# A transformer block on one core: one row of warm-up matmuls made longer, and part of the second layer norm moved between engines

## The chip, the cores and the metric

The kernel runs on one core of a Trainium2 chip. The metric is the device time of one execution, in microseconds (us). A profile of an execution also gives a span, from the first to the last instruction of the core; the device time is about 1.8 us longer than the span. The two must not be mixed.

Engines are named as in the profile: PE is TensorE (matmuls), PEld its weight loads, DVE VectorE, ACT ScalarE, POOL GpSimd, SP the engine that issues most DMAs.

## The reference, cut to what matters

```python
def reference(x, c, wqkv, wo, w_mod, w_fc1, w_fc2):     # B, N, D = 2, 256, 1152
    mod = (_silu(c) @ w_mod).reshape(B, 6, 1, D)
    shift_a, scale_a, gate_a, shift_m, scale_m, gate_m = [mod[:, i] for i in range(6)]
    h = _layernorm(x, axis=-1) * (1 + scale_a) + shift_a
    ...                                                  # q, k, v, attention, wo
    x = x + gate_a * a
    h2 = _layernorm(x, axis=-1) * (1 + scale_m) + shift_m      # "LN2"
    m = _gelu(h2 @ w_fc1) @ w_fc2                              # "FC1", "FC2"
    return x + gate_m * m
```

The 512 rows are four tiles (0 to 3) of 128; tiles 0 and 1 are batch 0, tiles 2 and 3 batch 1.

## The kernel before

At the start TensorE waits for the first weights (`w_scale_a`). A row of matmuls on zeros fills the wait and is meant to have its clock up when the work comes. In the profile of this kernel the row's matmuls start 0.43 us apart until the clock is released at 6.97 us, and 0.22 us apart from then on.

```python
    warm(2, pwarm)
    nc.tensor.transpose(pc[:], c_sb[:], ident[...])      # waits for c to land
    ...
    warm(14, pwarm)                                      # 128x128 by 128x512, on zeros
    act_stats()
    ...
    add0 = scale_group(0)                                # the first matmuls on w_scale_a
    ...
    k_step(0, 0, P)                                      # the first matmuls of K
```

In the second half each tile's `wo` output is gated (VectorE), added to x (GpSimd or VectorE), measured (VectorE), normalised, transposed by a DMA and modulated in place. The instructions stand on each engine in the order in which they are written here.

```python
    def ln2_modulate(b):
        for k in range(KD):                              # KD = 9 slices of 128 channels
            h = hT[:, k, b * N:(b + 1) * N]
            if k % 3 in ((1, 2) if b == 0 else (2,)):
                nc.scalar.activation(h, h, ACT.Identity, bias=shift_m[...], scale=scale_m[...])
            else:
                nc.vector.tensor_scalar(h, h, scale_m[...], shift_m[...], op0=ALU.mult, op1=ALU.add)

    def wo_group(t, i):                                  # tile t, column group i
        ...                                              # 9 matmuls into pacc
        nc.vector.tensor_tensor(tmp[:], pacc[:], gate_a[:, b, c0:c1], op=ALU.mult)
        (nc.gpsimd if i < 2 or t % TPB == 0 else nc.vector).tensor_tensor(
            x1[:, t, c0:c1], tmp[:], x_sb[:, t, c0:c1], op=ALU.add)
    ...
    ln2_stats(2, 1)
    ln2_modulate(0)
    wo_group(3, 0)
    ln2_stats(2, 2)
    ln2_sqrt(2)
    ...                                                  # the rest is in the diff below
    MSPLIT = 8
    for b in range(B):                                   # FC1: 8 panels for batch 0, then for batch 1,
        for m0 in range(0, MSPLIT, 2):                   # later panels for both batches at once
            ...
            if b == 0 and m0 == MSPLIT - 2:
                ln2_modulate(1)
```

## Time and profile before

| | before |
|---|---|
| timed runs, median of the first 3 | 245.29 us (245.05 to 245.33) |
| the profiled execution: device time | 246.9 us |
| the profiled execution: span | 245.04 us |
| TensorE busy | 97% of the span |

From the page of the kernel before. The last two lines cut the span into 40 slices: busy tenths of TensorE, and the clock that was granted to TensorE, in tenths of full speed.

```profile
span 245.0 us, 3884 instructions
...
PE 237.3 (97%) x1637; PEld 140.3 (57%) x1648; DVE 84.5 (34%) x198; ACT 65.5 (27%) x127; POOL 30.7 (13%) x46
...
PE   8789999999999999999999999999999999999994
...
PEclk9889999999999999999999999999999999999999
```

TensorE is the limit everywhere, and the two slices with a clock of 8 (6 to 18 us) stand out. The table of stretches shows them closer. Columns: stretch, its length, busy time of PE, PEld, DVE, ACT and POOL with the number of instructions, then the granted clock, the DMA share and GB/s.

```profile
8.00:9.00 1.00, 0.01 (x1) 0.02 (x2) 0.03 (x1) 0.00 (x0) 0.00 (x0) 1.00 1.10 352
10.00:11.00 1.00, 0.70 (x7) 0.57 (x7) 0.97 (x4) 0.65 (x3) 0.00 (x0) 0.69 1.15 323
11.00:12.00 1.00, 1.00 (x12) 1.00 (x10) 1.00 (x4) 1.00 (x4) 0.00 (x0) 0.50 1.11 334
12.00:13.00 1.00, 0.78 (x8) 0.72 (x8) 0.64 (x3) 0.77 (x2) 0.00 (x0) 0.50 1.20 306
13.00:14.00 1.00, 1.00 (x24) 1.00 (x24) 0.00 (x0) 0.00 (x0) 0.00 (x0) 0.60 1.16 316
```

TensorE idles from 8 to 9 us, and from 10.4 to 13.8 it runs at half clock. The waits of TensorE:

```profile
PE pm L221 <- DMA w_scale_a<-in_w_mod_dram: 1.2, 1, 1.2
...
PE pacc L706 <- DVE hT L599: 0.5, 1, 0.5
```

The first is the idle time at the start. The second is FC1's switch from batch 0 to batch 1, which waits for the modulates of batch 1. The timeline shows the VectorE work in front of it (start, duration, engine, line, operation, output and inputs):

```profile
96.62 1.20 DVE L599 TENSOR_SCALAR hT<-hT,scale_m,shift_m 128x256 bf16<-128x256 bf16 x3
...
99.89 8.02 PE L706 MATMUL pacc<-hT,w_f 128*128 128x256 bf16 x72
...
100.57 0.42 DVE L618 TENSOR_TENSOR x<-tmp,x_sb 128x256 f32<-128x256 f32 x1
...
101.69 0.29 DVE L618 TENSOR_TENSOR x<-tmp,x_sb 128x128 f32<-128x128 f32 x1
...
102.55 0.26 DVE L566 BATCH_NORM_AGGREGATE mv<-stats 128x2 f32<-128x24 f32 x1
...
108.41 5.81 PE L706 MATMUL pacc<-hT,w_f 128*128 128x256 bf16 x47 [0.50 <-DVE hT L599]
```

L599 are three modulates of batch 0, the two L618 are adds of tile 3, L566 aggregates tile 3's statistics. FC1 started at 99.89, so the aggregate began 2.66 us after it; the text calls this point the end of the statistics. Normalisation, transpose and modulates follow, and TensorE ran out of batch 0 before they were done.

### The profile page before, as it was taken

Reading aid. Unit: us, or ns where it says so; the run is one execution under the profiler, and the core shown is the slowest. Engines: PE = TensorE matmul, PEld = TensorE weight load, DVE = VectorE, ACT = ScalarE, POOL = GpSimd, SP = SyncE. Lnnn points to the kernel's source line nnn. Section 1 sums busy time; section 2 is a strip of 40 time slices with the busy share of each in tenths; the row PEclk is TensorE's granted clock in tenths of the full one; section 3 lists DMA queues with packets and bytes.
Section 4 is the critical chain, followed back from the end, with each engine's and each line's share of the span. In section 5 each row is a group of like instructions: output and inputs, shape, how many; then the busy total and the mean of one; then the engine's idle time right before and its main releaser. Section 6 shows DMA issues by size and latency. Waiting matters only on the chain.

```text
span 245.0 us, 3884 instructions
## 1 busy us (share of the span) xinstructions
PE 237.3 (97%) x1637; PEld 140.3 (57%) x1648; DVE 84.5 (34%) x198; ACT 65.5 (27%) x127; POOL 30.7 (13%) x46
## 2 busy tenths in 40 slices
PE   8789999999999999999999999999999999999994
PEld 2486444466666676878444444444665565566574
DVE  3752551214644677820000009999102000000001
ACT  7532351133524074482223322223000000000000
POOL 1000004000310514300000000000313221111111
PEclk9889999999999999999999999999999999999999
DMA  6999999999989972279999999999791000000000
GB/s 222 328 333 361 369 326 320 357 359 338 365 208 348 344 199 48 42 183 331 326 329 304 224 223 339 329 328 277 229 293 46 16 19 16 16 20 18 29 17 19
DMA packets 70813, 53.89 MB, mean 220 GB/s; under 512 B 18939, under 2 KB 65419, under 8 KB 70795
## 3 DMA queue, kind: packets, MB, share of 16 engines
q1 hardware_dynamic: 70064, 52.43, 72.9%
q0 software_dynamic: 704, 1.20, 1.6%
q8 instruction: 13, 0.21, 0.4%
q14 instruction: 5, 0.04, 0.1%
q10 hardware_dynamic: 27, 0.00, 0.0%
HBM read 48.08 MB, written 1.19 MB: 201 GB/s over the span
## 4 chain that ended last, share of the span: by engine, by line
PE 89%; DMA 4%; DVE 4%; issue 1%; ACT 1%; SPq 0%; DVEq 0%; ACTq 0%
PE pacc L766 29%; PE pacc L706 25%; PE pacc L503 7%; PE pacc L438 7%; PE pacc L612 6%; PE pk L253 5%; DMA w_scale_a<-in_w_mod_dram 3%; PE pk L282 2%; PE pn L365 1%; PE ps_s L458 1%; PE pa L530 1%; DMA hT<-xn 1%; PE pt L231 1%; DVE stats L624 1%; PE pm L221 1%
## 5 line engine op out<-in xcount | busy, mean ns | idle before, releaser
L706 PE MATMUL pacc<-hT,w_f 128*128 128x512 bf16 (+1 forms) x390 | 70.5, 340 | 0.8 <-DVE hT L599 0.5
L766 PE MATMUL pacc<-w_f,gT 128*128 128x384 bf16 (+2 forms) x468 | 70.5, 314 | 0.1
L766 PEld LDWEIGHTS <-gT 128*128 128x128 bf16 x468 | 44.3, 98 | 26.3
L706 PEld LDWEIGHTS <-w_f 128*128 128x128 bf16 x396 | 38.6, 98 | 32.4 <-issue 1.2
L429 DVE SCALAR_TENSOR_TENSOR late<-w_gate_mT,late 128x1152 bf16<-128x1152 bf16 x18 | 24.4, 1357 | 37.6 <-DMA w_gate_mT<-in_w_mod_dram 37.0
L772 DVE TENSOR_TENSOR tmp<-pacc,gate 128x384 f32<-128x384 f32 (+2 forms) x13 | 6.7, 525 | 63.0 <-PE pacc L766 50.5
L743 ACT ACTIVATE gT<-pacc 128x512 bf16<-128x512 f32 x28 | 16.7, 597 | 37.7 <-PE pacc L706 36.3
L612 PE MATMUL pacc<-w_o,big 128*128 128x384 bf16 (+2 forms) x117 | 18.1, 314 | 0.0
L503 PE MATMUL pacc<-w_v,hT 128*128 128x384 bf16 x108 | 17.9, 327 | 0.0
L774 POOL TENSOR_TENSOR o_sb<-tmp,x 128x384 bf16<-128x384 f32 (+1 forms) x12 | 11.6, 972 | 48.1 <-DVE tmp L772 48.1
L438 PE MATMUL pacc<-hT,w_q 128*128 128x512 bf16 x80 | 17.6, 380 | 0.1
L612 PEld LDWEIGHTS <-big 128*128 128x128 bf16 x117 | 10.9, 98 | 7.1 <-DVE big L270 0.6
L253 PE MATMUL pk<-big,w_k 128*128 128x256 bf16 (+2 forms) x88 | 14.2, 311 | 0.5 <-ACT big L240 0.4
L503 PEld LDWEIGHTS <-hT 128*128 128x128 bf16 x108 | 10.4, 98 | 7.2 <-issue 0.5
L438 PEld LDWEIGHTS <-w_q 128*128 128x128 bf16 x81 | 7.9, 98 | 9.6
L618 POOL TENSOR_TENSOR x<-tmp,x_sb 128x384 f32<-128x384 f32 x10 | 9.1, 911 | 18.8 <-DVE tmp L617 10.8
L420 POOL DMA_DIRECT2D gates_dram<-grow x4 | 2.0, 513 | 72.0 <-DVE grow L729 72.0
L253 PEld LDWEIGHTS <-w_k 128*128 128x128 bf16 x90 | 8.4, 107 | 3.5 <-issue 0.5
L617 DVE TENSOR_TENSOR tmp<-pacc,gate 128x384 f32<-128x384 f32 (+2 forms) x13 | 6.7, 518 | 4.8 <-PE pacc L612 4.7
L146 PE MATMUL pwarm<-zeros 128*128 128x512 bf16 x18 | 7.1, 557 | 1.2 <-DVE eps_t L92 1.2
L240 ACT ACTIVATE big<-pt,scale_a 128x256 bf16<-128x256 bf16 (+1 forms) x12 | 4.6, 434 | 11.1 <-PE pt L231 7.5
L420 POOL DMA_DIRECT2D s_dram<-s_rows x4 | 2.6, 654 | 35.9 <-DVE s_rows L423 35.9
(96 smaller groups left out, 150.8 us busy)
## 6 DMA issues: line engine op xcount, KB each, us to landing
w_f<-in_w_fc_dram SPq DMA_DIRECT2D x14, 864.0 KB, 11.0
w_f<-in_w_fc_dram SPq DMA_DIRECT2D x2, 2592.0 KB, 12.3
w_f<-in_w_fc_dram SPq DMA_DIRECT2D x2, 1728.0 KB, 15.1
w_shift_a<-in_w_mod_dram SPq DMA_DIRECT2D x3, 864.0 KB, 11.4
w_q<-in_wqkv_dram SPq DMA_DIRECT2D x3, 864.0 KB, 11.9
w_v<-in_wqkv_dram SPq DMA_DIRECT2D x3, 864.0 KB, 10.5
w_gate_a<-in_w_mod_dram SPq DMA_DIRECT2D x3, 864.0 KB, 10.0
w_o<-in_wo_dram SPq DMA_DIRECT2D x3, 864.0 KB, 13.8
```

The lines of the kernel that those rows point to most:

```text
L146: nc.tensor.matmul(dst[:], zeros[:, 0:P], zeros[:], start=True, stop=True)
L253: nc.tensor.matmul(pk[m][:, c0:c1], w_k[:, k, m * P:(m + 1) * P], hT0[:, k, c0:c1], start=(k == 0 and c0 == 0), stop=(k == KD - 1), skip_g ...
L429: nc.vector.scalar_tensor_tensor(spill, wT[:, j, :], 1.0, s_all[:, b, :], op0=ALU.mult, op1=ALU.mult, accum_out=dst[:, b * KD + j:b * KD + ...
L438: nc.tensor.matmul(pacc[:], w_q[:, k, m * P:(m + 1) * P], hT[:, k, :], start=(k == 0), stop=(k == KD - 1),)
L503: nc.tensor.matmul(pacc[:], hT[:, k, t * P:(t + 1) * P], w_v[:, k, pnl * PW:(pnl + 1) * PW], start=(k == 0), stop=(k == KD - 1),)
L612: nc.tensor.matmul(pacc[:], aT[:, k, t * P:(t + 1) * P], w_o[:, k, c0:c1], start=(k == 0), stop=(k == KD - 1),)
L617: nc.vector.tensor_tensor(tmp[:], pacc[:], gate_a[:, b, c0:c1], op=ALU.mult)
L618: (nc.gpsimd if i < 2 or t % TPB == 0 else nc.vector).tensor_tensor(x1[:, t, c0:c1], tmp[:], x_sb[:, t, c0:c1], op=ALU.add)
L706: nc.tensor.matmul(dst, w_f1[m // KD][:, k, ml * P:(ml + 1) * P], hT[:, k, c0:c1], start=(k == 0), stop=(k == KD - 1),)
L743: nc.scalar.activation(gT[:, m, :], pacc[:], ACT.Gelu_apprx_tanh)
L766: nc.tensor.matmul(pacc[:], gT[:, kk, t * P:(t + 1) * P], w_f2[j][:, r, c0 - n * PW:c0 - n * PW + cw], start=(kk == 0), stop=(kk == KF - 1),)
L774: (nc.vector if last else nc.gpsimd).tensor_tensor(o_sb[:], tmp[:], x1[:, t, c0:c0 + cw], op=ALU.add)
```

## The change

The intent: keep TensorE's clock up at the start with four more warm-ups; take work off VectorE in front of tile 3's statistics by moving all of batch 0's modulates to ScalarE and one add to GpSimd; run tile 3's statistics in one row; and shift tile 3's normalisation by 128 columns from ScalarE to VectorE.

```diff
-    warm(14, pwarm)
+    warm(18, pwarm)
...
-    def ln2_modulate(b):
-        for k in range(KD):
+    def ln2_modulate(b, ks=range(KD)):
+        for k in ks:
             h = hT[:, k, b * N:(b + 1) * N]
-            if k % 3 in ((1, 2) if b == 0 else (2,)):
+            if b == 0 or k % 3 == 2:
...
-        (nc.gpsimd if i < 2 or t % TPB == 0 else nc.vector).tensor_tensor(
+        (nc.vector if (t, i) in ((1, 2), (3, 3)) else nc.gpsimd).tensor_tensor(
...
     ln2_stats(2, 1)
-    ln2_modulate(0)
     wo_group(3, 0)
+    ln2_modulate(0, range(6))
     ln2_stats(2, 2)
     ln2_sqrt(2)
+    ln2_modulate(0, range(6, KD))
     wo_group(3, 1)
     ln2_stats(3, 0)
     ln2_recip(2)
     ln2_normalize(2)
     ln2_transpose(2)
     wo_group(3, 2)
+    wo_group(3, 3)
     ln2_stats(3, 1)
-    wo_group(3, 3)
     ln2_stats(3, 2)
     ln2_stats(3, 3)
     ln2_sqrt(3)
     ln2_recip(3)
-    ln2_normalize(3, 5 * P)
+    ln2_normalize(3, 4 * P)
     ln2_transpose(3)
```

## The prediction

> **What bounds it.** TensorE: 97% busy on the page, 89% of the chain that ended last. Only two places leave TensorE anything to gain.
>
> (a) Start. The 14 warm-up matmuls stop at about 7.8 us (timeline); TensorE idles 1.21 us until the first scale_a weights land at 8.95 (waits). In the table of stretches the granted clock is 1.00 until 10, 0.69 in 10-11, 0.50 in 11-13, 0.60 in 13-14, then 1.00: one slow stretch. [...] I count TensorE streaming about 35% of 6.97-10.38. In the slow stretch 128-column matmuls start every 107 ns, outside it every 55.
>
> (b) LN2, 95-110 us. Batch 0's part of FC1 ends with a matmul started at 107.64; the next starts at 108.41, and the first nine matmuls of batch 1 then take 1.28 us where 0.87 (8 x 0.109) is usual. Loss: 0.66 + 0.41 = 1.08 us. The chain through it is VectorE: three modulates of batch 0 (1.12 us), gating, adds, statistics of tile 3, root, normalisation (ends 104.6), transpose DMA (3.3 us), modulate.
>
> **What the change does.**
> 1. Four more warm-ups: at full clock 0.216 us each, they end near 8.65, before the weights (8.95): no delay. Streaming in the window 6.97-10.38 rises from 35% to about 60%. [...] I give 75% that the clock now stays at 1.00. Then 18 matmuls of K (1.92 to 1.0 us), one warm-up, four transposes save about 1.2 us. The second scale_a weights (landed 12.04) just allow it; later weights land at least 1 us ahead of use, so the gain should reach the end.
> 2. ScalarE takes three more modulates (0.51 us each, it had idle time); VectorE loses 1.12 us. ScalarE does six from 95.36 to 98.4, root of tile 2, three to about 100.2: just before FC1 needs them (99.9 to 100.8). Tile 2's normalisation starts about where it did (100.3).
> 3. The 256-column add (0.42 us) goes to GpSimd (estimate 0.62, from 0.91 for 384 columns), hidden behind the 128-column add and a statistic. Statistics run together.
> 4. Tile 3's normalisation splits 512/640 rather than 640/512: 0.1 us less on ScalarE.
>
> VectorE waits for TensorE's groups (97.14, 98.60), so not all of 1.12 + 0.42 returns: aggregate of tile 3 at about 101.8 (was 102.55), normalisation ends near 103.8 (104.60), transpose lands near 107.1 (107.92). Modulates of batch 1 still pace its first nine matmuls slightly (0.3 us lost): gain about 0.75 of 1.08.
>
> **Sum.** 245.29 - 0.9 (1.2 x 75%) - 0.75 = 243.6; 243.35 if the clock holds, 244.5 if not.
>
> Predicted 243.5 us, 8 in 10 between 242.9 and 244.6. Faster by over 2%: 0.005; within 2%: 0.99; slower: 0.005.
>
> **Signs.** Clock 1.00 throughout 10-14 us; second batch of scale_a matmuls starts near 12.1 (was 13.4); K's 256-column matmuls begin 1.2 us earlier. TensorE's gap before batch 1 of FC1 under 0.1 us; tile 3's transpose lands about 0.8 us earlier relative to FC1's start. FC2 unchanged (70.5 us).
>
> **What would make it wrong.** [...] the slow stretch moving to 13.8-17.2 (then the start gains nothing). ScalarE delivering batch 0's last slices late (FC1 stalls near 100 us), or delaying tile 2's transpose into tile 3's. GpSimd's add taking longer and holding up the statistics.

The 75% in the 0.9 is an estimate that rests on two counts for one trace: 35% of 6.97 to 10.38 us streamed before the change, about 60% expected after it.

## The result, and the profile after

| | before | after |
|---|---|---|
| timed runs, median of 6 | 245.32 us (245.05 to 245.79) | 245.06 us (244.60 to 245.92) |
| profiled execution, device time | 246.9 us | 244.82 us |
| profiled execution, span | 245.04 us | 243.06 us |

The ratio of the times is 0.9991, with a 95% interval of 0.9971 to 1.001. A ratio is the mean time of one kernel's fast runs over the mean of the other's of the same rounds, so it is not quite the ratio of the medians quoted. The measured 245.06 us lies outside the predicted range of 242.9 to 244.6.

The two profiles differ by 1.98 us and the timed runs by 0.26 us. Taken by itself the pair of profiles looks like a success of the prediction, which lay 1.8 us below the kernel before (243.5 against 245.29). The page after:

```profile
span 243.1 us, 3903 instructions
...
PE   8899999999999999999999999999999999999994
...
PEclk9999999999999999999999999999999999999999
```

The stretches at the start, with the clock in the third column from the right:

```profile
8.00:9.00 1.00, 0.49 (x19) 0.50 (x20) 0.03 (x1) 0.00 (x0) 0.00 (x0) 1.00 1.05 332
10.00:11.00 1.00, 1.00 (x19) 1.00 (x20) 0.97 (x4) 0.75 (x5) 0.00 (x0) 1.00 1.11 337
11.00:12.00 1.00, 1.00 (x26) 0.79 (x24) 0.97 (x3) 0.89 (x2) 0.00 (x0) 1.00 1.12 344
12.00:13.00 1.00, 0.60 (x16) 0.52 (x13) 0.91 (x6) 0.80 (x3) 0.00 (x0) 1.00 1.21 298
13.00:14.00 1.00, 1.00 (x13) 0.93 (x13) 0.25 (x1) 0.28 (x1) 0.00 (x0) 1.00 1.14 322
```

The clock is 1.00 in all of these stretches. The waits of TensorE:

```profile
...
PE pm L221 <- DMA w_scale_a<-in_w_mod_dram: 0.5, 1, 0.5
PE pk L253 <- ACT big L240: 0.4, 1, 0.4
...
```

The wait for `hT` is gone from the list, but its loss is not: TensorE still crawls at the switch, because the nine modulates come one by one: batch 1's first nine matmuls start within 1.29 us, where 0.87 is usual, and those that come late start about 0.05 us after their modulate has ended. The timeline in front of it:

```profile
98.40 13.84 PE L707 MATMUL pacc<-hT,w_f 128*128 128x256 bf16 x119
...
98.86 0.67 POOL L618 TENSOR_TENSOR x<-tmp,x_sb 128x256 f32<-128x256 f32 x1 [0.20 <-DVE tmp L617]
99.01 0.67 DVE L618 TENSOR_TENSOR x<-tmp,x_sb 128x128 f32<-128x128 f32 x1
...
99.60 1.07 DVE L624 BATCH_NORM_STATS2 stats<-x 128x6 f32<-128x384 f32 x3
100.70 0.27 DVE L566 BATCH_NORM_AGGREGATE mv<-stats 128x2 f32<-128x24 f32 x1
```

VectorE's 128-column add, 0.29 us before, now takes 0.67 us, and it runs beside GpSimd's add. Tile 3's statistics end 2.30 us after FC1's start; 1.91 was predicted, 2.66 it was.

A trace can be cut at two points: FC1's first matmul and FC2's first matmul. What follows FC2's start took 73.86 and 73.87 us in the two traces, so all of a difference is in the first two parts.

| us, from the traces | start to FC1 | FC1 to FC2 |
|---|---|---|
| before | 99.89 | 71.29 |
| after | 98.40 | 70.79 |

So the profiles say 1.49 us from the start and 0.50 us from the switch. The weights happened to land 0.48 us earlier in the profile after (8.46 against 8.94), which is about a third of the 1.49.

### The profile page after: what moved, and what is told of

Same layout as the page of the kernel before. It is cut to its first block, busy times and chain, and to the rows that moved or that the text cites. A ratio compares the mean times of both kernels' runs of the same rounds, so it can differ in the third digit from the quotient of the medians.

```text
span 243.1 us, 3903 instructions
## 1 busy us (share of the span) xinstructions
PE 237.1 (98%) x1652; PEld 139.4 (57%) x1652; DVE 83.7 (34%) x194; ACT 66.7 (27%) x130; POOL 31.3 (13%) x47
## 4 chain that ended last, share of the span: by engine, by line
PE 93%; DMA 3%; DVE 1%; SPq 0%; ACT 0%; issue 0%; DVEq 0%
PE pacc L707 29%; PE pacc L767 29%; PE pacc L612 7%; PE pacc L503 7%; PE pacc L438 7%; PE pk L253 4%; DMA w_scale_a<-in_w_mod_dram 3%; PE pk L282 2%; PE pn L365 1%; PE pa L530 1%; PE ps_s L458 1%; PE pm L221 1%; DVE stats L163 1%; PE pt L231 1%; PE pg L398 0%; SPq L85 0%
## 5 line engine op out<-in xcount | busy, mean ns | idle before, releaser
L503 PEld LDWEIGHTS <-hT 128*128 128x128 bf16 x108 | 10.4, 98 | 7.2 <-issue 0.5
L253 PE MATMUL pk<-big,w_k 128*128 128x256 bf16 (+2 forms) x90 | 13.4, 294 | 0.4 <-ACT big L240 0.4
L618 POOL TENSOR_TENSOR x<-tmp,x_sb 128x384 f32<-128x384 f32 (+1 forms) x11 | 9.8, 888 | 17.4 <-DVE tmp L617 10.7
L253 PEld LDWEIGHTS <-w_k 128*128 128x128 bf16 x90 | 7.5, 97 | 3.4 <-DMA w_k<-in_wqkv_dram 0.3
L146 PE MATMUL pwarm<-zeros 128*128 128x512 bf16 x23 | 7.7, 483 | 1.2 <-DVE eps_t L92 1.2
L595 ACT ACTIVATE hT<-hT,shift_m,scale_m 128x256 bf16<-128x256 bf16 x12 | 6.2, 588 | 3.8 <-DVE stats L624 3.3
## 6 DMA issues: line engine op xcount, KB each, us to landing
w_o<-in_wo_dram SPq DMA_DIRECT2D x3, 864.0 KB, 13.8
```

The lines of the kernel that those rows point to most:

```text
L146: nc.tensor.matmul(dst[:], zeros[:, 0:P], zeros[:], start=True, stop=True)
L253: nc.tensor.matmul(pk[m][:, c0:c1], w_k[:, k, m * P:(m + 1) * P], hT0[:, k, c0:c1], start=(k == 0 and c0 == 0), stop=(k == KD - 1), skip_g ...
L503: nc.tensor.matmul(pacc[:], hT[:, k, t * P:(t + 1) * P], w_v[:, k, pnl * PW:(pnl + 1) * PW], start=(k == 0), stop=(k == KD - 1),)
L618: (nc.vector if (t, i) in ((1, 2), (3, 3)) else nc.gpsimd).tensor_tensor(x1[:, t, c0:c1], tmp[:], x_sb[:, t, c0:c1], op=ALU.add)
```

## The experiments

The theory (A): the slow clock at 10.4 to 13.8 us was an accident of the profiled execution, which the timed runs rarely have; the true gain is the LN2 part alone. The main rival (B): the slow clock is there in every run, and its gain was lost elsewhere. A further suspicion (C, later called W): the four warm-ups cost time themselves. And for the LN2 part (L): GpSimd's add holds up VectorE's.

Each kernel was timed in five rounds beside the kernel before on the same chip. All gave correct results. The last two columns are from each kernel's profile, as differences of starts printed to 0.01 us.

| run | ratio (95% interval) | start to FC1 | FC1 to FC2 |
|---|---|---|---|
| before, again | 1.0006 (0.9994 to 1.0018) | 98.67 | 71.28 |
| 18 warm-ups only | 1.0023 (1.0006 to 1.0041) | 98.88 | 71.28 |
| LN2 part only | 0.9982 (0.9970 to 0.9995) | 98.25 | 70.78 |
| changed, both small adds on GpSimd | 0.9969 (0.9954 to 0.9984) | 98.50 | 70.37 |
| the same with 14 warm-ups | 0.9960 (0.9945 to 0.9975) | 98.32 | 70.38 |
| modulates moved only | 0.9990 (0.9968 to 1.0011) | 98.47 | 70.98 |
| before, nine panels | 1.0031 (1.0016 to 1.0047) | 98.39 | 72.18 |
| both adds, 14 warm-ups, nine panels | 0.9951 (0.9935 to 0.9968) | 98.73 | 70.13 |
| before, 22 warm-ups | 1.0060 (1.0039 to 1.0082) | 99.78 | 72.19 |
| before, 6 warm-ups | 1.0055 (1.0043 to 1.0067) | 99.85 | 71.28 |
| before, nine panels, 10 warm-ups | 1.0009 (0.9997 to 1.0021) | 99.75 | 70.33 |
| best, 10 warm-ups | 0.9991 (0.9978 to 1.0003) | 99.96 | 70.14 |

### The kernel before, again

No edit.

> The kernel before, once more, as it is. Theory A (the slow clock stretch at 10.4 to 13.8 us in the first profile of before was a rare or occasional event[...] and the timed runs mostly missed it): ratio 1.000 within 0.001; most timed runs have a span near 243.5 us and a granted clock of 0.997 or more; the new profile more likely than not shows a clock of 1.00 between 10 and 14 us. Theory B (14 warm-ups leave the stretch slow in every run, so the profile was typical): spans near 245.0 and clock near 0.993 in every run and in the profile.

Measured: ratio 1.0006, times 245.26 to 245.59. The second profile of the same kernel, its span and clock first, then two of the stretches:

```profile
core 0: 243.8 us, clock 1.000
```

```profile
11.00:12.00 1.00, 1.00 (x19) 0.88 (x17) 1.00 (x4) 1.00 (x4) 0.00 (x0) 1.00 1.11 334
12.00:13.00 1.00, 1.00 (x29) 0.93 (x27) 0.92 (x6) 0.69 (x2) 0.00 (x0) 1.00 1.20 304
```

The slow stretch is gone, without any change to the kernel, and the span is 243.8 rather than 245.0 us. Theory A held and B fell: 1.2 us of the difference between the first two profiles is a difference between two executions of one kernel. Of the 44 timed runs of the kernel before one is above 246 us (246.42). The clock recorded with the timed runs says the same: the first profile, with the stretch, has a mean clock of 0.993, and of the 38 timed runs with a clock on record that one alone has it; the others have 0.997 or more.

### 18 warm-ups only

```diff
-    warm(14, pwarm)
+    warm(18, pwarm)
```

> Only the four more warm-up matmuls, the rest as before. Theory A: ratio 0.999 to 1.001, since there is little to save in the runs that are timed. Theory B: 1.2 us less in each run, ratio 0.995. Rival C (four more warm-ups hold up the first scale_a matmuls in runs where the clock is released late): some single runs 0.3 to 1 us longer than the shortest, although their clock is 1.00.

Measured: ratio 1.0023, that is 0.56 us more; two of six runs at 246.4, the others at 245.4 to 245.8. The start in its profile:

```profile
3.16 0.19 PE L149 MATMUL pc<-ident,c_sb 18*128 18x18 bf16 x1 [0.93 <-DMA c_sb<-in_c_dram]
3.29 6.28 PE L146 MATMUL pwarm<-zeros 128*128 128x512 bf16 x18
9.40 0.59 PE L221 MATMUL pm<-sT,w_scale_a 128*128 128x2 bf16 x18
```

In this trace the first weights landed at 8.91, and TensorE took them up at 9.40: it was still warming up. Two things differ from the first profile. The row began at 3.29 us and not at 2.29, because it stands behind a transpose that waits for c to land; and the clock was released at 7.82 us and not at 6.97, so although the row began later, about as many of its matmuls (10 or 11) took 0.43 us rather than 0.22. Without the four (4 x 0.216 us) the row would have ended about 0.4 us before the weights landed (an estimate from this trace). In the two other profiles with 18 warm-ups the weights were taken up within 0.05 us, so the cost differs from run to run. FC1's part is 71.28 us as in the second profile of before, so nothing is lost at the switch. Theory A alone (no effect) is not enough; the suspicion C held.

### The LN2 part only

```diff
-    warm(18, pwarm)      # in the changed kernel
+    warm(14, pwarm)
```

> Only the LN2 part of the change, 14 warm-ups as before. Theory A: the LN2 part is all there is, 0.3 to 0.55 us less than before, ratio 0.998, and the same as the whole change within 0.3 us. Theory B: LN2 alone 0.5 us less, and the whole change would have to be 1.7 less. In the profile VectorE's 128-column add of tile 3 should again take about 0.67 us (0.29 before).

Measured: ratio 0.9982, that is 0.44 us less than before, and better than the whole change (0.9991, measured in other rounds). FC1's part is 0.50 us shorter, as with the whole change, and VectorE's 128-column add again takes 0.67 us. So A held: LN2 is all there is, and the warm-ups take some of it back.

### Both small adds on GpSimd

```diff
-        (nc.vector if (t, i) in ((1, 2), (3, 3)) else nc.gpsimd).tensor_tensor(
+        (nc.vector if (t, i) in ((1, 2),) else nc.gpsimd).tensor_tensor(
```

> The changed kernel, but the 128-column add of the last tile on GpSimd too. Theory L (VectorE's add of two SBUF inputs was blocked by GpSimd's add that ran at the same time: 0.67 us rather than 0.29): VectorE's statistics start 0.6 to 0.7 us earlier after FC1's start than in the changed kernel's profile, the aggregate of tile 3 0.4 us or more earlier (1.9 us after FC1's first matmul, not 2.3), tile 3's transpose lands 0.4 us earlier, and FC1's loss at the switch to batch 1 shrinks from about 0.55 us to 0.2: 0.3 to 0.4 us less than the changed kernel, ratio 0.997. Rival (the statistics wait for GpSimd's adds whatever VectorE does): aggregate within 0.15 us of the changed kernel's.

Measured: ratio 0.9969. The timeline:

```profile
98.50 5.73 PE L707 MATMUL pacc<-hT,w_f 128*128 128x256 bf16 x51
...
98.97 1.06 POOL L618 TENSOR_TENSOR x<-tmp,x_sb 128x256 f32<-128x256 f32 x2 [0.20 <-DVE tmp L617]
99.00 1.36 DVE L624 BATCH_NORM_STATS2 stats<-x 128x6 f32<-128x384 f32 x3
...
100.39 0.26 DVE L566 BATCH_NORM_AGGREGATE mv<-stats 128x2 f32<-128x24 f32 x1
```

FC1 started at 98.50 here, so the statistics start 0.50 us after it (1.20 with the change as it was) and end 1.89 us after it (2.30). FC1's part shrinks by a further 0.42 us. Theory L held: the 0.38 us by which VectorE's add had grown came back when that add left VectorE. The rival was right in part: the row of statistics takes 1.36 us rather than 1.07, for its second and third begin (99.68, 100.07) only when GpSimd's two adds have ended (99.64, 100.03). That wait of 0.29 us costs less than the earlier start of 0.70 us gains.

How the one add held up the other is not shown beyond the times. In the trace of the changed kernel VectorE's add began 0.15 us after GpSimd's and ended 0.15 us after it, at 99.68 against 99.53. Those 0.15 us are less than the 0.29 us that the add takes alone, so a part of it had passed before; which, the trace does not say. GpSimd's 256-column add took 0.67 us beside VectorE's, and 0.67 us without it in this run. Nor was it adds alone, or all of VectorE's work: in the trace of the kernel before, a modulate that began 0.31 us after an add on GpSimd took 0.69 us (0.33 to 0.35 for the others) and ended 0.08 us after it, while a statistic beside the next add (98.21) took 0.55 us, as one without an add beside it did (100.92).

### The same with 14 warm-ups

```diff
-    warm(18, pwarm)      # in the kernel of the last experiment
+    warm(14, pwarm)
```

> The LN2 part with both of tile 3's small adds on GpSimd, but 14 warm-ups as before. Theory W (the four added warm-ups cost about 0.2 to 0.5 us on average, because in most runs the clock is released later than in the first profile, or the first warm-ups start later, and the longer row then ends after the weights have landed): ratio 0.995 to 0.996, 0.3 to 0.5 us less than the same kernel with 18 warm-ups (0.9969), and less spread among its runs. Theory N (warm-ups make no difference, the 0.23 per cent of the run with them alone was chance): 0.9969 again. In the profile the first scale_a matmul starts within 0.1 us of its weights' landing.

Measured: ratio 0.9960, and the spread among six runs is 0.5 us (244.33 to 244.85) instead of 1.2. The first weights landed at 8.62, the first matmul on them began at 8.67. Theory W fits, but this pair alone would not prove it: the intervals of 0.9960 and 0.9969 overlap, and the two were timed on different chips. The evidence is the run with 18 alone, whose interval excludes 1, and that all three pairs with and without the four have the same sign; the run with 22 below adds to it.

### The modulates moved only

```diff
...
-            if k % 3 in ((1, 2) if b == 0 else (2,)):
+            if b == 0 or k % 3 == 2:
...
-    ln2_modulate(0)
     wo_group(3, 0)
+    ln2_modulate(0, range(6))
     ln2_stats(2, 2)
     ln2_sqrt(2)
+    ln2_modulate(0, range(6, KD))
```

> Of the change only the move of batch 0's modulates to ScalarE; the 256-column add stays on VectorE, the statistics stay apart, 640/512 split, 14 warm-ups. Theory L (GpSimd's add saved VectorE 0.43 us and cost it 0.38 by blocking its other add): tile 3's aggregate 2.4 us after FC1's first matmul (2.30 with the whole change, 2.66 before), time within 0.25 us of the run with the whole LN2 part, ratio 0.998 to 0.999. Rival (the add on GpSimd was worth its 0.43 us): aggregate at 2.65 or later, no gain over before.

Measured: the statistics end 2.40 us after FC1's start (2.30 with the whole LN2 part, 2.66 before), FC1's part is 70.98.

```profile
98.47 5.73 PE L707 MATMUL pacc<-hT,w_f 128*128 128x256 bf16 x51
...
100.86 0.26 DVE L566 BATCH_NORM_AGGREGATE mv<-stats 128x2 f32<-128x24 f32 x1
```

The ratio, 0.9990, has an interval that includes 1, so the verdict rests on the trace. Of the 0.36 us that the LN2 part took off this point, 0.26 came from the modulates, and 0.10 from everything else, the add on GpSimd included. The add on GpSimd, with the other add left on VectorE, gained almost nothing: 0.42 us taken off VectorE, 0.38 us given back by the one held up.

### The kernel before with nine panels ahead of the switch

```diff
-    MSPLIT = 8
+    MSPLIT = 9           # the ninth panel alone in its accumulator
...
```

A panel is 128 of FC1's output channels: nine matmuls for one batch, 0.98 us.

> The kernel before with nine instead of eight of FC1's panels done for batch 0 ahead of batch 1; nothing of the change in it. If what the LN2 part can win is only the 1.08 us for which TensorE stands or crawls at the switch to batch 1, then 0.98 us more work ahead of the switch covers 0.7 to 0.85 us of it without moving anything off VectorE: ratio 0.9965 to 0.997, a larger gain than the whole change. If the loss is elsewhere: ratio 1.000.

Measured: ratio 1.0031, slower in all six runs (246.08 to 246.47). The expectation failed. TensorE waited 1.4 us at the switch:

```profile
PE pacc L706 <- DVE hT L599: 1.4, 1, 1.4
```

The chain of work names the transpose of tile 3, which took 5.13 us where 3.29 was usual:

```profile
103.14 5.13 DMA hT<-xn
```

The transpose is carried out in 16 parts that report one by one. In this trace 15 of them reported between 106.56 and 106.70, and the last at 108.27. The kernel issues the same loads of `w_f` there as the kernel before; what is new is one packet in the table of DMA queues for 106.0 to 107.5:

```profile
q8 instruction: 1, 0.02, 4.0%
```

It is a 16 KB fetch of instructions, at 106.23, which took 0.95 us. The profile names the queue q8 "instruction"; the two profiles of before and after have 13 packets of 16 KB each on it, which took 0.95 to 1.34 us. In the kernel before the fetch in question comes at 111 to 113 us, after the switch.

### Nine panels with 10 warm-ups

```diff
-    warm(14, pwarm)      # in the kernel with nine panels
+    warm(10, pwarm)
```

> The kernel before with nine panels, but 10 warm-ups, so that TensorE's instruction stream is 8 instructions shorter ahead of FC1. Theory F (in the nine-panel run a 16 KB instruction fetch at 106.23 us held one of the 16 DMA engines while tile 3's transpose ended, and that one of its 16 parts came 1.6 us after the others): if the shift moves the fetch out of that place, all 16 parts land within 0.15 us, 3.3 us after the issue, and the time is 0.7 us below before or more, ratio 0.995 to 0.998; if the fetch stays in place, so does the late part and the ratio of 1.003. Rival (nine panels are slower for another reason): ratio 1.003 with all 16 parts on time.

Measured: the fetch moved to 112.20, all 16 parts reported between 107.66 and 107.77. The time from issue to landing of the LN2 transposes (three of the four; the profile gives no landing for tile 2's), first with 14 warm-ups, then with 10:

```profile
DMA to landing us min/median/max: 3.2/3.4/5.1
```

```profile
DMA to landing us min/median/max: 3.2/3.2/3.3
```

FC1's part is 70.33 us, 0.95 less than before. This part of theory F held; that the fetch and the late part were on one DMA engine is not shown. The ratio did not (1.0009, expected 0.995 to 0.998): with 10 warm-ups the slow clock came back at 9.97 to 13.39 in the profile, and the start to FC1 took 99.75 us. Four of the five timed runs have a mean clock of 0.990 or 0.993. I had brought in a second effect with the means by which I moved the first. A direct timing of nine panels with the fetch out of the way and the clock up is missing; the next run is the nearest to it.

### Both adds, 14 warm-ups, nine panels

No new edit: the kernel of the fifth experiment with the nine panels of the seventh.

> Both: the LN2 part with both small adds on GpSimd, 14 warm-ups, and nine panels ahead of the switch. No gap above 0.13 us at the switch; 0.2 to 0.3 us less than the same with eight panels, about 1.1 to 1.3 us less than before, ratio 0.995. If it equals the kernel before with nine panels within 0.1 per cent, moving LN2 work is not worth having beside the ninth panel.

Measured: ratio 0.9951, median 244.32 against 245.40. FC1's matmuls follow each other through the switch without a gap over 0.13 us, and FC1's part is 70.13. This version beats both kernels; against the one with eight panels it gains 0.25 us in the trace, while the intervals of the two ratios overlap. The instruction fetch came at 107.48 here, after the transpose had landed (105.86). That is luck of placement, and should be looked at again after any edit.

### 22 and 6 warm-ups

```diff
-    warm(14, pwarm)
+    warm(22, pwarm)      # and, in another run, warm(6, pwarm)
```

> The kernel before with 22 warm-ups: the suspected cost doubled. Theory W (each warm-up that ends after the first weights have landed costs its 0.216 us): 0.9 to 1.4 us more than before, ratio 1.004 to 1.006 (1.0023 was measured for 18), the first scale_a matmul 0.9 us or more after its weights' landing in the profile. Theory N (no effect): ratio within 0.001 of 1.000.

Measured for 22: ratio 1.0060. The first matmul on the weights began at 10.30, 1.56 us after they landed, and FC1 started 1.1 us later than in the second profile of before. But FC1's part was longer too, by 0.91 us: an instruction fetch at 105.56 fell into tile 3's transpose again, and this time all 16 parts landed 0.92 us late (4.18 rather than 3.26 us after the issue). So the ratio overstates the cost of the warm-ups; theory W rests on the first part only.

> The kernel before with 6 warm-ups, to bring the slow clock on. If the slow stretch costs what the first profile of before shows (246.9 beside 245.3 in the timed runs, 1.6 us): most runs at 246.5 to 247.5 us with granted clocks of 0.99 or a late release, ratio 1.004 to 1.008, and matmuls every 107 ns at some point between 9 and 16 us. If the clock does not matter there (the weights' arrival hides it): ratio 1.000.

Measured for 6: ratio 1.0055, 246.44 to 247.12 in all runs. The timeline shows K's 128-column matmuls:

```profile
10.59 2.13 PE L253 MATMUL pk<-big,w_k 128*128 128x128 bf16 x18
```

They take 2.13 us; in the profile after, at full clock, 1.17. Yet the table of stretches says 1.00 in the clock column:

```profile
11.00:12.00 1.00, 1.00 (x13) 1.00 (x11) 1.00 (x3) 1.00 (x4) 0.00 (x0) 1.00 1.11 332
```

The clock was released for the first time at 13.57 us in this trace; six more of these matmuls took 0.49 us from 13.87 us on, as in the profile after (0.49 from 12.07). What lies before the first record of the clock is counted as 1.00, though the matmuls ran at half speed. The start to FC1, 99.85, is as long as in the executions with the slow stretch (99.89, 99.75, 99.96); the six profiles with 14 warm-ups and without it have 98.25 to 98.73. So the slow clock costs about 1.4 us when it comes.

### The best version with 10 warm-ups

```diff
-    warm(14, pwarm)      # in the kernel with both adds on GpSimd and nine panels
+    warm(10, pwarm)
```

> The best version so far (both small adds on GpSimd, nine panels; ratio 0.9951) with 10 warm-ups instead of 14. Theory W with the clock's lottery: no gain left from ending earlier, since with 14 the first scale_a matmul starts within 0.1 us of its weights in most runs, and the slow clock becomes more frequent: one or more runs of six about 1.5 us longer with a clock of 0.993; ratio 0.995 to 0.998. If fewer are simply better: ratio 0.994 or less.

Measured: ratio 0.9991, all five runs between 244.97 and 245.87. The slow clock was more frequent: the profile has it (10.53 to 13.94), and three of the five runs have a mean clock of 0.990 to 0.993. But no run comes down to the other version's median of 244.32; the two with a clock of 1.000 took 244.97 and 244.98, and what held them up is not shown. With 6 and 10 warm-ups the time is worse, with 18 and 22 too; of the numbers tried 14 is the best placed.

## Why the prediction was wrong

**Bounds, point (a): the reading was right for that one execution and wrong for the kernel.** The prediction says "one slow stretch" and builds on it. The stretch was real and cost what was said (1.2 us between two profiles of one kernel). But it was in the profiled execution (246.9 us) and hardly ever in the timed ones (245.05 to 245.33; one of 38 later ones). The time of the profiled execution stood beside the profile, and the prediction does not mention it.

**Step 1, "save about 1.2 us", weighed with 75%: this is the step that failed.** The chance was put on whether the change would remove the slow stretch. It should have been put on whether the stretch was there to be removed. If it failed, the prediction counted on no gain (244.5), and not on a cost. Measured, the four warm-ups alone cost 0.56 us (ratio 1.0023). The argument "they end near 8.65, before the weights (8.95): no delay" took the start of the row (2.29 us) and the release of the clock (6.97 us) from one execution. Both move: in the eleven profiles with 14 warm-ups or more the row starts at 2.29 to 3.32 us, in eight of them at 3.05 or later, and the clock was released anywhere between 5.09 and 8.37.

**Step 2, the modulates on ScalarE: right.** ScalarE delivered in time, FC1 did not stall at its start, and tile 2's normalisation started 0.26 us after FC1's first matmul (0.42 before).

**Step 3, the add to GpSimd "hidden behind the 128-column add": the size failed, and the reason is in the word hidden.** GpSimd's add took 0.67 us (0.62 estimated). But running beside VectorE's add it held it up, 0.29 to 0.67 us. The prediction's gain at the switch was 0.75 us; 0.50 was measured in the trace and 0.44 in the time. With both adds on GpSimd the statistics end 1.89 us after FC1's start, which is the 1.91 of the prediction (101.8 against 99.89), and the gain is 0.91 us.

**Step 4, the split of the normalisation: right**, 0.81 us rather than 0.92 on ScalarE.

**Sum.** Predicted: -0.9 - 0.75. Measured one by one: +0.56 - 0.44; together in one kernel -0.26 by the medians of six runs. The single effects are each uncertain by 0.3 to 0.4 us, so their sum of +0.12 and the measured value agree as well as they can.

**What stays open.** How busy TensorE has to be for its clock to stay up was not measured, nor when that is decided. In the first profile the clock was halved 3.41 us after its release (10.38 against 6.97), and for 3.41 us (to 13.79). Counting the columns that TensorE streamed (0.216 us for 512 columns, 0.055 for 128) in the 3.41 us that followed the release of the clock, it was then halved at about 17%, 28% and 35% (three executions) and kept up at about 44% (the modulates moved only) and 48% (the second profile of before). These are five executions and not a rule; a share of busy time would not sort them, as TensorE was busy for 58% of those 3.41 us in the first profile, where the clock was halved, and for 52% with the modulates moved only, where it was kept. That the late part of the transpose and the instruction fetch shared a DMA engine is not shown; it is inferred from two executions with both and one in which moving the fetch removed the delay; the trace does not say which engine carried which packet. Other transposes speak against a simple rule: with 18 warm-ups only, a fetch at 90.14 fell into tile 0's transpose, which landed 3.19 us after its issue as usual; in the profile after, tile 0's transpose took 4.12 us from 86.97, and was overdue before the fetch there began at 90.56. So a fetch need not delay a transpose, and something else can.

## What to carry to other kernels

Set the time of the profiled execution beside the timed runs before reading anything from the profile; if it is off by about as much as the gain that you hope for (here 1.6 us for a hoped 1.8), take a second profile and trust only what both show. A filler that is meant to end before an event must be judged by the spread of its start, its speed and the event over several executions. When work is moved from VectorE to GpSimd, ask what VectorE does in those microseconds: an add of its own there gave the gain back here (0.42 us taken off, 0.38 given back).
